# Weight sums moved between plain FFN2 tiles, one PV copy on ScalarE, and halved last stores in a sigmoid attention + SwiGLU kernel

## The chip, the cores and the metric

The kernel runs on one core of a Trainium2 chip. The metric is device time in microseconds (us) for one launch, as the median of several runs; the profile is of one execution and its span is from the first to the last instruction.

## The reference

```python
def _attn_ref(q, k, v):                       # each (8, 12, 448, 64) float32
    S = q.shape[2]
    scale = 1.0 / np.sqrt(q.shape[-1])
    scores = scale * np.matmul(q, k.transpose(0, 1, 3, 2)) - np.log(S)
    attn = 1.0 / (1.0 + np.exp(-scores))
    return np.matmul(attn, v)

x = attn_out.transpose(0, 2, 1, 3).reshape(B * S, H * D)   # (3584, 768)
g = x @ w_gate                                # (768, 1536)
silu = g * (1.0 / (1.0 + np.exp(-g)))
val = x @ w_val                               # (768, 1536)
out = silu * val @ w_out                      # (1536, 768)
```

Attention with a sigmoid in place of the softmax, over 8 batches of 12 heads, then one gated feed-forward block over all 3584 tokens.

## The kernel before, in words

**Attention.** Work goes by head groups n = 0 to 23: batch b = n // 3, four heads each. For each n and each of C = 7 chunks c of the keys, `qk_tile` makes the scores with four 64x64 matmuls (L207) and `sig_tile` takes their sigmoid on ScalarE (L225, or L222 in two halves, one per PSUM bank). When all seven chunks of an n are there, `pv` makes the product with v in 28 matmuls (L238) and three VectorE copies to the fp16 tiles xT: one of 128 partitions from the first bank (L247), two of 64 partitions from the second (L255). Only the PV of n=2, in the ramp, puts those two on ScalarE (L253). q and k come to their transposed form by DMA (`load`), a cast on GpSimd (L159) and, from n=6 on, a DMA transpose that SP issues (L167).

**FFN1.** For each batch and each of NF = 12 blocks f, `ffn1` makes gate and value in 12 matmuls (L266) into the two banks of one PSUM tile; ScalarE makes the sigmoid s (L284), VectorE the gate product t (L286) and the hidden block hT (L290).

**FFN2.** It is done for a pair of batches at once (`pb` = 0 to 3), in seven output tiles of 128 tokens by 768. Tile 6 is plain: `ffn2`, 24 matmuls (L459), two scaled copies on VectorE (L472), two stores (L479). The tiles g and g+3 are done together by `ffn2_group`, a Strassen-like form with seven half products of six matmuls each (42, L387) in place of 48. It takes sums of hidden blocks, made by `h_sums` and `make_sums` on VectorE in every odd batch (L349), and eight sums of weight blocks wT (four kinds for each of two pairs s of weight tiles), made once by `w_sum` (L319). Between products, `snap` (L398) copies a bank's partial sum out and `put` (L404) adds a bank to an output tile; TensorE goes on in the other bank meanwhile, and into the same bank only after the snapshot. The order of products is 1, 2, 6, 5, 7, 3, 4 in banks 0, 1, 0, 1, 0, 1, 0. Kinds 1 to 4 of the weight sums serve products 5, 6, 7 and 4.

**PSUM.** Four tiles of two banks are handed out in turn (`Banked`): each score tile, PV, FFN1 unit and FFN2 tile or group takes the next, so a user waits for the readers of the one four back. `read` and `write` tell the framework that work on different banks of a tile is independent. For readers of one tile on two engines that nothing is declared for, the framework puts one behind the other.

**Order.** The order of instructions on each engine is the order of the program text. A planner lays it out: `units` is a list of FFN1 blocks, weight sums and FFN2 tiles with planned durations (2.26 for an FFN1 block, 3.9 for a plain tile, 6.83 for a group, 0 for sums), and `visits` a list of attention steps of four or three chunks (visit (n, 0): chunks 0 to 3; visit (n, 4): 4 to 6), each with a due time. Before each unit, if the planned clock `tcur` has reached the due time of the next visit, that visit is put in: the score matmuls of two chunks, any PV that has become complete, the two sigmoids, then the rest (L519). A visit also brings the loads, casts and transposes of later groups (`plan`): visit (n, 0) the transposes of n+1 from n=9 on. Due times of batch 2 and after depend on the end of batch 0's FFN1 alone.

Before the change the eight weight sums stand in `units` between the FFN1 blocks of batch 1, from f=3 to f=11 (L484, L493).

**The end.** The last group of the last pair stores its first output tile o1 in two parts of 64 tokens and full width (L426) after its last product is in the program, then the second half of the columns of o2 (L430), all on SP. The first half of o2's columns is scaled by ScalarE for 64 tokens (L443) and by VectorE for the other 64 (L447), into tiles of their own, and stored from ScalarE's and SP's queues (L449).

Of the kernel before, what the change touches and what calls it, by code (L numbers as in the profile page):

```python
# [9 lines left out]
FP32 = mybir.dt.float32  # L10
# [3 lines left out]
MULT = mybir.AluOpType.mult  # L14
# [5 lines left out]
def kernel(  # L20
# [10 lines left out]
    nc = tc.nc  # L31
    ctx.enter_context(tc.manual_schedule())

    B, H, S, D = q.shape
    DM = H * D
    DFF = moe_w_gate.shape[1]
    C = S // D
# [6 lines left out]
    HREC = 1.0 / HSC  # L44
# [33 lines left out]
    class Banked:  # L78
# [28 lines left out]
        def read(self, ins, bank):  # L107
            if bank is not None:
                if self.has_mm[1 - bank]:
                    tc.declare_no_dep(ins.ins, group=self.mm[1 - bank], reason="the other bank")  # L110
                self.has_rd[bank] = True
                tc.add_to_no_dep_group(self.rd[bank], ins.ins)


    FW = 3
# [109 lines left out]
            nc.scalar.activation(out=pt, in_=sc[:, :, :S], func=SIGM, bias=sb_t, scale=qkscale)  # L225
        pts[(n, c)] = pt

    def pv(n, two=False, at=None):
        b, j = divmod(n, NJ)
        P = Banked(at=at).t  # L230
        vt = v16.pop(n)
        for c in range(C):
            pt = pts.pop((n, c))
            for h2 in range(2):
                for w in range(2):
                    r = slice(w * 64, w * 64 + 64)
                    g = (w ^ h2) * 64
                    nc.tensor.matmul(  # L238
                        out=P[g:g + 64, h2, :S],
                        lhsT=vt[r, h2, c * D:(c + 1) * D],  # L240
                        rhs=pt[r, h2, :],
                        start=(c == 0),
                        stop=(c == C - 1),
                    )

        x = xtp.tile([128, S], FP16, tag="xT", name=f"xT_{b}_{2 * j}")
        nc.vector.tensor_copy(out=x, in_=P[:, 0, :S])  # L247
        xT[(b, 2 * j)] = x
        x = xtp.tile([128, S], FP16, tag="xT", name=f"xT_{b}_{2 * j + 1}")
        for w in range(2):  # L250
            o, i = x[w * 64:(w + 1) * 64, :], P[(1 - w) * 64:(2 - w) * 64, 1, :S]
            if two:
                nc.scalar.copy(out=o, in_=i)  # L253
            else:
                nc.vector.tensor_copy(out=o, in_=i)  # L255
        xT[(b, 2 * j + 1)] = x


    hT = {}
# [88 lines left out]
                a, b, op = a12, hS[(pb, 2, i)], SUB  # L348
            nc.vector.tensor_tensor(out=t, in0=a, in1=b, op=op)  # L349

    def out_rows(pb, m):
        dsts = []
        for i in range(2):
            bb, c = divmod(2 * m + i, C)
            bb += 2 * pb
            dsts.append(out[bb * S:(bb + 1) * S, :].rearrange("(p c) n -> c p n", c=C)[c])
        return dsts

    def ffn2_group(pb, g):

        D = Banked("o")
        cs = slice(g * 128, (g + 1) * 128)

        def h_of(f, m):
            f1 = lambda i: i // FW * 2 * FW + i % FW + f
            return lambda i: (hT[(pb, f1(i))].rearrange("p b s -> p (b s)")[:, m * 128:(m + 1) * 128], f1(i))

        def s_of(kind):
            return lambda i: (hS[(pb, kind, i)][:, cs], None)

        def w_of(s, h):
            return lambda i: wo16[2 * (i // FW) + s][:, i % FW, h * hw:(h + 1) * hw]

        def t_of(kind):
            return lambda i: wT[(kind, i // FW)][:, i % FW, :]

        prods = {
            1: (h_of(0, g), w_of(0, 0)), 2: (h_of(FW, g), w_of(1, 0)), 3: (s_of(4), w_of(1, 1)),
            4: (h_of(FW, g + 3), t_of(4)), 5: (s_of(1), t_of(1)), 6: (s_of(2), t_of(2)), 7: (s_of(3), t_of(3)),
        }  # L380

        def mm(k, bank, first, last):
            A, B_ = prods[k]
            for i in range(HF):
                l, f = A(i)
                D.write(
                    nc.tensor.matmul(  # L387
                        out=D.t[:, bank, :hw], lhsT=l, rhs=B_(i), start=(first and i == 0), stop=(i == HF - 1),
                        skip_group_check=True,
                    ),  # L390
                    bank,
                    uses=(pb, f),
                )

        def snap(bank, o, half):
            o = o[:, half * hw:(half + 1) * hw]
            D.read(
                nc.vector.tensor_scalar(out=o, in0=D.t[:, bank, :hw], scalar1=HREC, scalar2=None, op0=MULT), bank  # L398
            )

        def put(bank, o, half):
            i = D.t[:, bank, :hw]
            o = o[:, half * hw:(half + 1) * hw]
            D.read(nc.vector.scalar_tensor_tensor(out=o, in0=i, scalar=HREC, in1=o, op0=MULT, op1=ADD), bank)  # L404

        last = pb == B // 2 - 1
        end = last and g == 2
        o1 = osp.tile([128, DM], FP32, tag="osb", name="osb")
        mm(1, 0, True, False)
        snap(0, o1, 0)  # L410
        mm(2, 1, True, True)
        put(1, o1, 0)
        mm(6, 0, False, False)
        snap(0, o1, 1)
        mm(5, 1, True, False)
        o2 = osp.tile([128, DM], FP32, tag="osb", name="osb")
        snap(1, o2, 1)
        mm(7, 0, False, False)
        put(0, o2, 1)
        mm(3, 1, False, True)  # L420
        put(1, o1, 1)
        mm(4, 0, False, True)
        eng = nc.sync
        dsts = out_rows(pb, g)
        for i in range(2):
            eng.dma_start(out=dsts[i], in_=o1[i * 64:(i + 1) * 64, :])  # L426
        dsts = out_rows(pb, g + 3)
        if end:
            for i in range(2):
                eng.dma_start(out=dsts[i][:, hw:], in_=o2[i * 64:(i + 1) * 64, hw:])  # L430
            last_half(D, 0, [d_[:, :hw] for d_ in dsts])
        else:
            snap(0, o2, 0)
            for i in range(2):
                eng.dma_start(out=dsts[i], in_=o2[i * 64:(i + 1) * 64, :])

    def last_half(D, bank, dsts):

        for i in range(2):
            r = slice(i * 64, i * 64 + 64)  # L440
            oe = stg.tile([128, 2, S], FP32, tag="stg", name=f"oe{i}").rearrange("p a b -> p (a b)")[:, :hw]
            if i == 0:
                ev = nc.scalar.activation(  # L443
                    out=oe[r], in_=D.t[r, bank, :hw], func=mybir.ActivationFunctionType.Copy, scale=HREC
                )
            else:
                ev = nc.vector.tensor_scalar(out=oe[r], in0=D.t[r, bank, :hw], scalar1=HREC, scalar2=None, op0=MULT)  # L447
            D.read(ev, bank)
            (nc.scalar if i == 0 else nc.sync).dma_start(out=dsts[i], in_=oe[r])  # L449

    def ffn2(pb, m):
        D = Banked("o")
# [17 lines left out]
        for half in range(2):  # L470
# [3 lines left out]
                ),  # L474
                half,
            )
        dsts = out_rows(pb, m)
        for i in range(2):
            nc.sync.dma_start(out=dsts[i], in_=osb[i * 64:(i + 1) * 64, :])  # L479


    FU1, FU2, FU3 = 2.26, 3.9, 6.83
    units = []
    t_at = {(1, 3 + i + i // 4): (i // 4, (3, 2, 1, 4)[i % 4]) for i in range(8)}  # L484
    f1_start, f1_end = {}, {}
    tt = 0.0
    for pb in range(B // 2):
        for b in (2 * pb, 2 * pb + 1):
            f1_start[b] = tt
            for f in range(NF):  # L490
                if b or f > 2:
                    units.append((FU1, ffn1, (b, f)))
                if (b, f) in t_at:  # L493
                    units.append((0.0, w_sum, t_at[(b, f)]))
                tt += FU1
            f1_end[b] = tt
        o_units = [(0.0, make_sums, (99,)), (FU2, ffn2, (pb, C - 1))]
        for g in range(3):
            o_units.append((FU3, ffn2_group, (pb, g)))
        units += o_units  # L500
        tt += sum(u[0] for u in o_units)
# [14 lines left out]
        else:  # L516
            vtime.append(FIRST + 3.5 + (b - 2 + frac) * PER)

    def attn_step(group, pvs):  # L519
        for part in (group[:2], group[2:]):  # L520
            scs = [(n, c, qk_tile(n, c)) for n, c in part]
            while pvs:
                pv(pvs.pop(0))
            for i, (n, c, sc) in enumerate(scs):

                sig_tile(n, c, sc, split=len(group) == 4 and part[0] == group[0] and i == 1)

    NPE = 2 * NJ

# [89 lines left out]
    chunk(2, 6)  # L619
    early.append(Banked("f"))  # L620
    ffn1_mm(early[1], 0, 1, range(NP - 2))
    pv(2, two=True, at=(k0 + 1) % 4)
    early.append(Banked("f", at=(k0 + 2) % 4))
    ffn1_mm(early[2], 0, 2, range(NP - 2))
    for f, Df in enumerate(early):
# [31 lines left out]
    for dur, fn, args in units:  # L657
        if vi < len(visits) and tcur >= vtime[vi]:
            group = visits[vi]
            vi += 1  # L660
            pvs, pend = pend, []
            attn_step(group, pvs)
            for n, c in group:
                for act, of in plan.get((n, c), ()):
                    act(of)
                if c == C - 1:
                    pend.append(n)
            while post:
                trans_pe(post.pop())
# [39 lines left out]
```

## Time and profile before

| what | value |
|---|---|
| three runs | 422.71, 422.71, 422.18 us |
| profiled execution | 422.16 us, span 420.4 us, clock 0.995 |
| FFN1 matmuls L266 | 1152, 353 and 352 ns each, pipelined |
| weight sums L319 | 8 in 6.2 us, 79.5 to 105.5 us |
| group matmuls L387 | 504 |
| plain tile matmuls L459 | 96, 3.9 us for 24 |
| PV copies L247, L255 | 24 and 46, 623 and 622 ns each |
| PV copies L253 on ScalarE | 2, 526 ns each |
| batch 1's FFN1, 64.6 to 102.5 us | TensorE busy 35.97 of 37.90, VectorE 31.33 |
| batch 3's FFN1, 166.9 to 201.5 us | TensorE busy 34.38 of 34.60, VectorE 24.95 |

A row of the profile names a source line, an engine and an operation, then output<-inputs by the program's names, then the shape. A matmul's length is from its start to its modelled end, and matmuls overlap, so the length of a run of them is less than their number times one. In an order of time, each row has its start, its length and, in brackets, how long its engine had stood idle and what ended that.

### The profile page before, as it was taken

Reading aid. Unit: us, or ns where it says so; the run is one execution under the profiler, and the core shown is the slowest. Engines: PE = TensorE matmul, PEld = TensorE weight load, DVE = VectorE, ACT = ScalarE, POOL = GpSimd, SP = SyncE. Lnnn points to the kernel's source line nnn. Section 1 sums busy time; section 2 is a strip of 40 time slices with the busy share of each in tenths; the row PEclk is TensorE's granted clock in tenths of the full one; section 3 lists DMA queues with packets and bytes.
Section 4 is the critical chain, followed back from the end, with each engine's and each line's share of the span. In section 5 each row is a group of like instructions: output and inputs, shape, how many; then the busy total and the mean of one; then the engine's idle time right before and its main releaser. Section 6 shows DMA issues by size and latency. Waiting matters only on the chain.

```text
span 420.4 us, 7928 instructions
## 1 busy us (share of the span) xinstructions
PE 404.7 (96%) x3189; PEld 210.7 (50%) x3189; DVE 259.8 (62%) x477; ACT 211.8 (50%) x291; POOL 95.7 (23%) x125
## 2 busy tenths in 40 slices
PE   6899999989999999999999999999999999999994
PEld 2544545445555445445555445444555544555562
DVE  2726647789565556677664556568656447578653
ACT  4976885745344565565333865665444552222000
POOL 5564242457030355030012345020000000000000
PEclk9899999999999999999999999999999999999999
DMA  8999999999469997341167998310045400000134
GB/s 299 228 274 222 212 183 224 178 215 174 124 143 236 188 163 191 84 111 23 37 122 200 179 236 209 74 24 0 2 107 144 102 2 1 2 0 2 37 95 131
DMA packets 59141, 54.39 MB, mean 129 GB/s; under 512 B 35680, under 2 KB 52448, under 8 KB 59104
## 3 DMA queue, kind: packets, MB, share of 16 engines
q0 software_dynamic: 18880, 30.94, 34.3%
q1 hardware_dynamic: 39872, 22.39, 25.9%
q8 instruction: 25, 0.41, 0.4%
q10 hardware_dynamic: 352, 0.56, 0.4%
q14 instruction: 12, 0.10, 0.1%
HBM read 47.19 MB, written 11.01 MB: 138 GB/s over the span
## 4 chain that ended last, share of the span: by engine, by line
PE 83%; DVE 7%; ACT 6%; issue 2%; DMA 1%; DVEq 0%; ACTq 0%
PE ps_D L266 47%; PE ps_D L387 19%; PE ps_D L207 7%; PE ps_D L238 7%; ACT pt L225 4%; PE ps_D L459 4%; DVE t L286 2%; DVE xT L255 1%; DVE hT L290 1%; DMA st<-in_q_dram 1%; PE ps_D L181 1%; ACT s L284 1%; DVE xT L247 1%; DVE S L349 1%; DVE wT L319 1%
## 5 line engine op out<-in xcount | busy, mean ns | idle before, releaser
L225 ACT ACTIVATE pt<-ps_D,sb_t 128x896 f16<-128x896 f32 x148 | 140.3, 1014 | 85.8 <-PE ps_D L207 85.6
L266 PE MATMUL ps_D<-xT,wg 128*128 128x448 f16 x576 | 126.9, 353 | 2.5 <-DVE t L286 1.8
L266 PE MATMUL ps_D<-xT,wv 128*128 128x448 f16 x576 | 126.4, 352 | 0.0
L286 DVE TENSOR_TENSOR t<-ps_D,s 128x448 f16<-128x448 f32 x96 | 59.8, 623 | 70.8 <-ACT s L284 70.3
L284 ACT ACTIVATE s<-ps_D 128x448 f16<-128x448 f32 x96 | 52.6, 548 | 84.8 <-PE ps_D L266 72.4
L266 PEld LDWEIGHTS <-wg 128*128 128x128 f16 x576 | 53.6, 98 | 60.5 <-issue 15.0
L266 PEld LDWEIGHTS <-wv 128*128 128x128 f16 x576 | 56.4, 98 | 52.9 <-issue 0.3
L159 POOL CAST c<-st 128x896 bf16<-128x896 f32 (+1 forms) x42 | 39.7, 956 | 128.5 <-DMA T<-c 70.7
L290 DVE SCALAR_TENSOR_TENSOR hT<-ps_D,t 128x448 f16<-128x448 f32 x96 | 60.0, 625 | 10.4 <-DVE t L286 0.5
L207 PE MATMUL ps_D<-T,T 64*64 64x448 bf16 x672 | 46.8, 361 | 3.5 <-ACT T L190 1.1
L398 DVE TENSOR_SCALAR osb<-ps_D 128x384 f32<-128x384 f32 x47 | 26.2, 558 | 21.0 <-PE ps_D L387 20.6
L387 PEld LDWEIGHTS <-S 128*128 128x128 f16 x288 | 28.2, 98 | 20.1 <-issue 1.7
L387 PE MATMUL ps_D<-wT,S 128*128 128x384 f16 x216 | 37.0, 326 | 0.8 <-DVE osb L398 0.8
L238 PE MATMUL ps_D<-pt,v 64*64 64x448 f16 x672 | 36.0, 349 | 0.5 <-ACT pt L225 0.5
L207 PEld LDWEIGHTS <-T 64*64 64x64 bf16 x672 | 16.1, 106 | 27.2 <-issue 19.8
L247 DVE CAST xT<-ps_D 128x448 f16<-128x448 f32 x24 | 15.0, 623 | 23.6 <-PE ps_D L238 18.2
L255 DVE CAST xT<-ps_D 64x448 f16<-64x448 f32 x46 | 28.6, 622 | 0.8
L404 DVE SCALAR_TENSOR_TENSOR osb<-ps_D,osb 128x384 f32<-128x384 f32 x36 | 20.1, 558 | 13.7 <-PE ps_D L387 13.3
L387 PEld LDWEIGHTS <-hT 128*128 128x128 f16 x216 | 20.5, 98 | 15.8 <-issue 2.9
L149 POOL DMA_DIRECT2D v<-in_v_dram x24 | 17.6, 731 | 41.1 <-PE ps_D L207 41.0
L238 PEld LDWEIGHTS <-v 64*64 64x64 f16 x672 | 19.8, 107 | 12.8 <-issue 1.5
L387 PE MATMUL ps_D<-wo,hT 128*128 128x384 f16 x144 | 25.4, 326 | 0.0
(40 smaller groups left out, 195.3 us busy)
## 6 DMA issues: line engine op xcount, KB each, us to landing
out_dram<-osb SPq DMA_DIRECT2D x54, 192.0 KB, 2.9
st<-in_q_dram POOLq DMA_DIRECT2D x20, 448.0 KB, 4.7
st<-in_k_dram POOLq DMA_DIRECT2D x20, 448.0 KB, 5.7
v<-in_v_dram POOLq DMA_DIRECT2D x24, 224.0 KB, 7.8
wg<-in_moe_w_gate_dram POOLq DMA_DIRECT2D x4, 576.0 KB, 14.4
wv<-in_moe_w_val_dram POOLq DMA_DIRECT2D x4, 576.0 KB, 14.6
wo<-in_moe_w_out_dram POOLq DMA_DIRECT2D x4, 576.0 KB, 11.1
st<-in_q_dram SPq DMA_DIRECT2D x4, 448.0 KB, 6.0
```

The source lines that it names most:

```text
L159: (eng.copy if eng is nc.scalar else eng.tensor_copy)(out=t.rearrange("p c h d -> p h c d"), in_=st.rearrange("p h (c d) -> p h c d", c=C) ...
L207: nc.tensor.matmul(out=sc[w * 64:(w + 1) * 64, h2, :S], lhsT=kt[r, w * 64:(w + 1) * 64], rhs=qt[r, :, w * 64:(w + 1) * 64], start=True, st ...
L225: nc.scalar.activation(out=pt, in_=sc[:, :, :S], func=SIGM, bias=sb_t, scale=qkscale)
L238: nc.tensor.matmul(out=P[g:g + 64, h2, :S], lhsT=vt[r, h2, c * D:(c + 1) * D], rhs=pt[r, h2, :], start=(c == 0), stop=(c == C - 1),)
L255: nc.vector.tensor_copy(out=o, in_=i)
L266: nc.tensor.matmul(out=D.t[:, i, :S], lhsT=w16[f // FW][:, pr, cs], rhs=xT[(b, pr)], start=(pr == 0), stop=(pr == NP - 1),),
L284: D.read(nc.scalar.activation(out=s16, in_=D.t[:, 0, :S], func=SIGM), 0)
L286: D.read(nc.vector.tensor_tensor(out=t1, in0=D.t[:, 0, :S], in1=s16, op=MULT), 0)
L290: nc.vector.scalar_tensor_tensor(out=hT[(b // 2, f)][:, b % 2, :], in0=D.t[:, 1, :S], scalar=HSC, in1=t1, op0=MULT, op1=MULT),
L387: nc.tensor.matmul(out=D.t[:, bank, :hw], lhsT=l, rhs=B_(i), start=(first and i == 0), stop=(i == HF - 1), skip_group_check=True,),
L398: nc.vector.tensor_scalar(out=o, in0=D.t[:, bank, :hw], scalar1=HREC, scalar2=None, op0=MULT), bank
L404: D.read(nc.vector.scalar_tensor_tensor(out=o, in0=i, scalar=HREC, in1=o, op0=MULT, op1=ADD), bank)
```

## The change: what it does

Four edits, in one diff.

- The weight sums leave FFN1 of batch 1. FFN2 of the first pair now has three plain tiles (6, 0, 3) and the groups 1 and 2 only. Three sums stand after tile 6, three after tile 0, two after tile 3, ahead of group 1. Groups stay as they are in the other pairs.
- `pv` takes `how`: 0 puts all three copies on VectorE, 2 both half copies on ScalarE (the PV of n=2, as before), 1 one half copy on ScalarE, after the sigmoids of the step's first two chunks. A visit ahead of an FFN1 block uses 0, any other visit 1.
- `apart` declares that a reader of a PSUM tile need not stand behind named readers of it (another bank or other partitions). It is used for `how` = 1 and for the last two scaled copies.
- In the last group, o1 is stored in two halves of columns: the first after `put(1, o1, 0)`, the second at the end. The half of o2 is stored right after `put(0, o2, 1)`.

```diff
+    def apart(second, *firsts):
+        for first in firsts:
+            keys[0] += 1
+            tc.add_to_no_dep_group(f"half{keys[0]}", first.ins)
+            tc.declare_no_dep(second.ins, group=f"half{keys[0]}", reason="another bank or other partitions")
...
-        nc.vector.tensor_copy(out=x, in_=P[:, 0, :S])
+        first = nc.vector.tensor_copy(out=x, in_=P[:, 0, :S])
...
+        halves = [(x[w * 64:(w + 1) * 64, :], P[(1 - w) * 64:(2 - w) * 64, 1, :S]) for w in range(2)]
+        done = [nc.vector.tensor_copy(out=o, in_=i) for o, i in halves[how:]]
+        if how == 2:
+            for o, i in halves:
                 nc.scalar.copy(out=o, in_=i)
...
+        def rest():
+            if how == 1:
+                o, i = halves[0]
+                apart(nc.scalar.copy(out=o, in_=i), first, *done)
+
+        return rest
...
         put(1, o1, 0)
+        if end:
+            store((nc.sync, nc.sync), pb, g, o1, lo)
         mm(6, 0, False, False)
         snap(0, o1, 1)
...
         put(0, o2, 1)
+        if end:
+            store((nc.sync, nc.sync), pb, g + 3, o2, hi)
         mm(3, 1, False, True)
         put(1, o1, 1)
         mm(4, 0, False, True)
...
+        store((nc.sync, nc.sync), pb, g, o1, hi)
...
+            store_half(nc.scalar if w == 0 else nc.sync, pb, g + 3, w, oe, lo)
+        apart(evs[1], evs[0])
...
-    t_at = {(1, 3 + i + i // 4): (i // 4, (3, 2, 1, 4)[i % 4]) for i in range(8)}
...
-                if (b, f) in t_at:
-                    units.append((0.0, w_sum, t_at[(b, f)]))
...
         o_units = [(0.0, make_sums, (99,)), (FU2, ffn2, (pb, C - 1))]
-        for g in range(3):
+        if pb == 0:
+            ts = [(0.0, w_sum, (s, kind)) for s in range(2) for kind in (3, 2, 1, 4)]
+            o_units += ts[:3] + [(FU2, ffn2, (pb, 0))] + ts[3:6] + [(FU2, ffn2, (pb, 3))] + ts[6:]
+        for g in range(1 if pb == 0 else 0, 3):
             o_units.append((FU3, ffn2_group, (pb, g)))
...
             scs = [(n, c, qk_tile(n, c)) for n, c in part]
-            while pvs:
-                pv(pvs.pop(0))
+            rest = [pv(pvs.pop(0), how) for _ in range(len(pvs))]
             for i, (n, c, sc) in enumerate(scs):
                 sig_tile(n, c, sc, split=len(group) == 4 and part[0] == group[0] and i == 1)
+            for f in rest:
+                f()
...
-    pv(2, two=True, at=(k0 + 1) % 4)
+    pv(2, how=2, at=(k0 + 1) % 4)
...
-            attn_step(group, pvs)
+            attn_step(group, pvs, 0 if fn is ffn1 else 1)
```

More of the change, by code (lines that the diff above doesn't have):

```diff
@@ L226, in sig_tile, with pv @@
         pts[(n, c)] = pt
-    def pv(n, two=False, at=None):
+    def pv(n, how=0, at=None):
         b, j = divmod(n, NJ)
@@ L246, in pv @@
         x = xtp.tile([128, S], FP16, tag="xT", name=f"xT_{b}_{2 * j}")
-        nc.vector.tensor_copy(out=x, in_=P[:, 0, :S])
+        first = nc.vector.tensor_copy(out=x, in_=P[:, 0, :S])
         xT[(b, 2 * j)] = x
         x = xtp.tile([128, S], FP16, tag="xT", name=f"xT_{b}_{2 * j + 1}")
-        for w in range(2):
-            o, i = x[w * 64:(w + 1) * 64, :], P[(1 - w) * 64:(2 - w) * 64, 1, :S]
-            if two:
-                nc.scalar.copy(out=o, in_=i)
-            else:
-                nc.vector.tensor_copy(out=o, in_=i)
-        xT[(b, 2 * j + 1)] = x
+        xT[(b, 2 * j + 1)] = x
+        halves = [(x[w * 64:(w + 1) * 64, :], P[(1 - w) * 64:(2 - w) * 64, 1, :S]) for w in range(2)]
+        done = [nc.vector.tensor_copy(out=o, in_=i) for o, i in halves[how:]]
+        if how == 2:
+            for o, i in halves:
+                nc.scalar.copy(out=o, in_=i)
+        def rest():
[3 more added lines that the diff above has]
+        return rest
     hT = {}
@@ L349, in make_sums, with store, store_half @@
             nc.vector.tensor_tensor(out=t, in0=a, in1=b, op=op)
[L351 to L357, printed above, removed]
+    def store(engs, pb, m, osb, cols):
+        for w in range(2):
+            store_half(engs[w], pb, m, w, osb, cols)
+    def store_half(eng, pb, m, w, osb, cols):
+        bb, c = divmod(2 * m + w, C)
+        bb += 2 * pb
+        d = out[bb * S:(bb + 1) * S, cols].rearrange("(p c) n -> c p n", c=C)[c]
+        eng.dma_start(out=d, in_=osb[w * 64:(w + 1) * 64, cols])
     def ffn2_group(pb, g):
@@ L404, in put @@
             D.read(nc.vector.scalar_tensor_tensor(out=o, in0=i, scalar=HREC, in1=o, op0=MULT, op1=ADD), bank)
-        last = pb == B // 2 - 1
-        end = last and g == 2
+        end = pb == B // 2 - 1 and g == 2
+        lo, hi, both = slice(0, hw), slice(hw, DM), slice(0, DM)
         o1 = osp.tile([128, DM], FP32, tag="osb", name="osb")
@@ L422, in ffn2_group @@
         mm(4, 0, False, True)
[L423 to L432, printed above, removed]
-            snap(0, o2, 0)
[L434 to L442, printed above, removed]
+        if not end:
+            store((nc.sync, nc.sync), pb, g, o1, both)
+            snap(0, o2, 0)
+            store((nc.sync, nc.sync), pb, g + 3, o2, both)
+            return
+        store((nc.sync, nc.sync), pb, g, o1, hi)
+        evs = []
+        for w in range(2):
+            r = slice(w * 64, w * 64 + 64)
+            oe = stg.tile([128, 2, S], FP32, tag="stg", name=f"oe{w}").rearrange("p a b -> p (a b)")
+            if w == 0:
                 ev = nc.scalar.activation(
-                    out=oe[r], in_=D.t[r, bank, :hw], func=mybir.ActivationFunctionType.Copy, scale=HREC
+                    out=oe[r, :hw], in_=D.t[r, 0, :hw], func=mybir.ActivationFunctionType.Copy, scale=HREC
                 )
             else:
-                ev = nc.vector.tensor_scalar(out=oe[r], in0=D.t[r, bank, :hw], scalar1=HREC, scalar2=None, op0=MULT)
-            D.read(ev, bank)
-            (nc.scalar if i == 0 else nc.sync).dma_start(out=dsts[i], in_=oe[r])
+                ev = nc.vector.tensor_scalar(out=oe[r, :hw], in0=D.t[r, 0, :hw], scalar1=HREC, scalar2=None, op0=MULT)
+            D.read(ev, 0)
+            evs.append(ev)
+            store_half(nc.scalar if w == 0 else nc.sync, pb, g + 3, w, oe, lo)
+        apart(evs[1], evs[0])
     def ffn2(pb, m):
@@ L476, in ffn2 @@
             )
-        dsts = out_rows(pb, m)
-        for i in range(2):
-            nc.sync.dma_start(out=dsts[i], in_=osb[i * 64:(i + 1) * 64, :])
+        store((nc.sync, nc.sync), pb, m, osb, slice(0, DM))
     FU1, FU2, FU3 = 2.26, 3.9, 6.83
     units = []
-    t_at = {(1, 3 + i + i // 4): (i // 4, (3, 2, 1, 4)[i % 4]) for i in range(8)}
     f1_start, f1_end = {}, {}
@@ L517, with attn_step @@
             vtime.append(FIRST + 3.5 + (b - 2 + frac) * PER)
-    def attn_step(group, pvs):
+    def attn_step(group, pvs, how):
         for part in (group[:2], group[2:]):
             scs = [(n, c, qk_tile(n, c)) for n, c in part]
-            while pvs:
-                pv(pvs.pop(0))
+            rest = [pv(pvs.pop(0), how) for _ in range(len(pvs))]
             for i, (n, c, sc) in enumerate(scs):
                 sig_tile(n, c, sc, split=len(group) == 4 and part[0] == group[0] and i == 1)
+            for f in rest:
+                f()
     NPE = 2 * NJ
```

## The prediction

> **What bounds the kernel now.** I read the page's busy times and its chain first, then the wait table of TensorE (PE), then the order of time around each of its waits, then the tail. The busy row and the chain:
>
> ```profile
> PE 404.7 (96%) x3189; PEld 210.7 (50%) x3189; DVE 259.8 (62%) x477; ACT 211.8 (50%) x291; POOL 95.7 (23%) x125
> PE 83%; DVE 7%; ACT 6%; issue 2%; DMA 1%; DVEq 0%; ACTq 0%
> ```
>
> TensorE is busy for 96% of the 420.4 us span and carries 83% of the chain. So there are only three ways to move the time: matmuls added or removed, idle holes of TensorE closed or opened, and the stretch after the last matmul. The wait table gives the holes; these three lines are those after the ramp that come from VectorE (DVE), in total us, count, longest (a fourth, of 0.2, is in the ramp):
>
> ```profile
> PE ps_D L266 <- DVE t L286: 1.8, 3, 1.3
> PE ps_D L387 <- DVE osb L398: 0.8, 4, 0.2
> PE ps_D L207 <- DVE hT L290: 0.6, 1, 0.6
> ```
>
> Where they lie: 0.60 at 81.6 and 1.33 at 91.1, both in FFN1 of batch 1; 0.24, 0.18, 0.17 and 0.24 in FFN2 (118.7, 216.8, 308.1, 325.3); 0.22 at 170.3 and at 235.0. That is 3.2 us in all. The two large ones in order of time (start, length, instruction, idle before it in brackets):
>
> ```profile
> 79.50 0.75 DVE L319 TENSOR_TENSOR wT<-wo,wo 128x1152 f16<-128x1152 f16 x1
> ...
> 81.57 0.57 PE L207 MATMUL ps_D<-T,T 64*64 64x448 bf16 x8 [0.60 <-DVE hT L290]
> ...
> 89.74 0.75 DVE L319 TENSOR_TENSOR wT<-wo,wT 128x1152 f16<-128x1152 f16 x1
> 90.41 0.62 DVE L286 TENSOR_TENSOR t<-ps_D,s 128x448 f16<-128x448 f32 x1
> 91.08 1.29 PE L266 MATMUL ps_D<-xT,wg 128*128 128x448 f16 x6 [1.33 <-DVE t L286]
> ```
>
> A weight sum (wT) stands on VectorE just ahead of the gate product t or hT that TensorE needs before it may refill a PSUM tile. From 77 to 91 us VectorE is busy 12.9 of 14.0 us, and four sums (4 x 0.75 = 3.0) are part of that. The FFN2 hole and the tail:
>
> ```profile
> 116.76 1.26 DVE L255 CAST xT<-ps_D 64x448 f16<-64x448 f32 x2
> 118.05 0.56 DVE L398 TENSOR_SCALAR osb<-ps_D 128x384 f32<-128x384 f32 x1
> ...
> 118.66 3.08 PE L387 MATMUL ps_D<-wT,S 128*128 128x384 f16 x18 [0.24 <-DVE osb L398]
> ```
> ```profile
> 415.56 0.55 ACTq L449 DMA_DIRECT2D out_dram<-oe  x1
> 415.62 0.56 DVE L447 TENSOR_SCALAR oe<-ps_D 64x384 f32<-64x384 f32 x1 [1.04 <-ACT oe L443]
> 415.77 1.25 SPq L430 DMA_DIRECT2D out_dram<-osb  x2
> 417.12 0.54 SPq L449 DMA_DIRECT2D out_dram<-oe  x1
> ```
>
> In the first, the snapshot L398 stands behind three PV copies of 0.62. In the second, the last store leaves SP at 417.12, behind four others (two of L426 from 414.61, two of L430); it lands 2.2 us later, and the span ends 1.05 after that.
>
> **What the Trainium skill says.** "PSUM — Partial Sum Buffer", section "Engine vs sequencer instructions": ScalarE and VectorE queues are strict FIFO. The trace agrees: L398 runs only after the copies ahead of it. Same page, "PSUM bank collisions raise a hardware error": two engines may be in one bank at once if they touch different 32-partition quadrants. The new paired readers do, since each takes 64 partitions; no row of before shows such a pair together (DVE L447 waits 1.04 for ACT L443). "DMA: Bandwidth & Descriptors", section "Issuing engines are not separate DMA queues": several issuers save only issue time. In the tail that is 0.47 to 0.62 a store on SP.
>
> **The change part by part**, against the span of 420.4.
>
> 1. *Weight sums leave batch 1: −1.93.* All eight (6.2 us of L319) go. First hole: without the sum at 79.50, t and hT end 0.7 earlier, near 80.85, and TensorE is busy with PV until 80.97: hole 0. Second: with four sums fewer ahead of it, t is bound by its sigmoid instead. Following the rows: QK at 80.97, its sigmoids to 83.4, then s, t, hT and two S sums (0.36 each) per unit bring the t in question to its end near 88.7, while TensorE would want it at 89.15. Hole 0, slack 0.4. So 0.60 + 1.33 = 1.93 (bounds 0.9 and 1.93). The inputs keep up: the tightest operand of this stage, the transposed k of n=7, landed 5.6 us before use.
>
> 2. *Three plain tiles: +0.97.* Group 0 of the first pair (7 products x 6 = 42 matmuls) becomes tiles 0 and 3 (2 x 24 = 48). A plain tile takes 3.90 us in the chain (L459 x24), a group 6.83: 2 x 3.90 − 6.83 = +0.97, all on TensorE. VectorE evacuations fall from seven of 0.56 to four of 0.55, which is beside it. SP gets four stores of 192 KB either way.
>
> 3. *The sums' new place: +0.84.* Six of eight run on VectorE while TensorE has 3.9 us per tile for 2 x 0.55 of evacuation: 1.1 + 3 x 0.75 = 3.35 fits, at no cost. The last two (kinds 1 and 4 of the second pair) do not. Working through the planner, visit (9,0), with PV of n=8, falls just before them. So VectorE's queue reads PV copy, PV half copy, sum, sum, snapshot L398, and TensorE's third product waits for that snapshot. By the rows at 116: first copy from 116.10 to 116.73, half copy to 117.38, two sums to 118.88, L398 to 119.45, TensorE at 119.5. It could start at 118.66 − 0.24 = 118.42. Hole 1.08 in place of 0.24: +0.84. Queued behind it are only the following put and snapshots, which catch up inside the group. Bounds 0.3 and 1.1.
>
> 4. *One PV half copy on ScalarE in FFN2: −0.59.* Three of the four PVs there lose 0.62 on VectorE, more than the holes of 0.18, 0.17, 0.24 (the fourth is in 3). On ScalarE the copy costs 0.53 (row L253); it stands behind the split sigmoid and delays the next two by 0.53. Their PSUM tiles are wanted only after a tile or group of 4 to 7 us, and the timeline shows ScalarE idle 4.8 to 8.7 before each of these visits. Cost 0, bounds 0 and 0.2.
>
> 5. *The planner's clock: +0.4.* The extra 0.97 is added to tcur after FFN2 of pair 0, while due times stay. A visit moves up when its lateness at the unit before was negative by less than 0.97. Visits (11,0), (11,4), (13,0), (13,4), (17,0), (17,4), (19,0), (19,4), the lone last PV by one FFN1 unit; (15,0) by one group; (21,0) past ffn2. Their transposes, SP's queue included, have slack of 6.6 us and more, except n=17: k landed at 237.78 for a use at 239.58. That visit (due 162.39; tcur 161.78 a unit earlier becomes 162.75) now wants it at 237.22, that is 5.6 us after the first of its two transposes is issued (231.60, behind FFN2's last stores). That pair took 6.2; the five other pairs issued behind stores took 4.8 to 6.4. So bounds 0 and 0.8, value 0.4. For (21,0), QK could wait up to 0.2 on the last hT; I take 0. The two holes of 0.22 stay.
>
> 6. *Tail: −1.1.* The first half of o1 is stored at about 410.9 and o2's half at 413.6, under matmuls. After 414.6 SP issues two half stores of o1 (to about 416.0), then the last one at 416.05 instead of 417.12; the DVE reading no longer waits for ACT (from 415.05 instead of 415.62) and is ready by then. It lands at 418.27 by its own 2.2; ACT's store landed at 418.23. Before: 419.34. So 1.07 earlier (bounds 0.8 and 1.3).
>
> Sum: −1.93 + 0.97 + 0.84 − 0.59 + 0.4 − 1.1 = **−1.4**: span 419.0. That profiled execution took 422.16 with its span of 420.4; the three timed runs are 422.71, 422.71 and 422.18. I apply it to the median: **421.3**.
>
> **The rivals.** *A, batch 1 has a second limiter.* If t is then held by its sigmoid behind three score sigmoids (2.8 us on ScalarE), only about half of 1.93 comes back: −0.4, 422.3, no change that can be told. For it: ScalarE's idle before s is short there (0.6 to 1.7). Against: the estimate left 0.4 of slack, and later odd batches, with the same sums of h and no wT, show one hole of 0.22.
>
> *B, slower: the early half store holds its own tile.* L398's second snapshot writes the other columns of o1 while the store of the first columns is in flight. If the program orders them as one tile, that snapshot waits for the landing: second half issued near 411.4, landing 2.6 later, 414.0, instead of starting at 411.10. TensorE's product 7 waits for it: +2.7, total +1.3, **424.0**. It decides only if the wait is there at all; the columns are disjoint, and no row of before has a write to a part of a tile whose other part a DMA is reading.
>
> *C, less is lost.* The n=17 transposes land in time, and the sums cost their lower bound: −0.4 − 0.54 more: −2.3, 420.4.
>
> *D, moved visits open holes that I priced at 0* (at (21,0), (19,0), or a late load): +1.5 or more beyond the forecast, 422.8 and up.
>
> **How the numbers follow.** About 0.2% (0.85 us) can be told from no change. Forecast 0.55, A 0.17, B 0.08, C 0.12, D 0.08. Faster: forecast and C, 0.67. Slower: B and half of D, 0.12. Same: the rest, 0.21. The range leaves out B and D's far end. Low end: C, the tail's 1.3 in place of 1.1, and half of the 0.5 between the three runs: 420.36 − 0.2 − 0.25 = 419.9. High end: A with step 5 at its 0.8 and step 4 at its 0.2: 422.3 + 0.4 + 0.2 = 422.9.
>
> **What would show it.** No L319 rows before FFN2 and no VectorE waits of TensorE between 77 and 92; 144 of L459's matmuls instead of 96; a TensorE wait on the osb snapshot near 1.1 in the first group after the plain tiles and none at the other three FFN2 visits; a TensorE wait on T of 0 to 0.8 before visit (17,0); SP's last store about 1.1 after the last matmul instead of 2.1. I am wrong if the batch 1 holes remain, if the snapshot wait of step 3 is absent or twice as long, or if an L398 in the last group waits on a DMA.

## The result, and the profile after

| | before | changed |
|---|---|---|
| median of 4 runs | 422.63 us | 420.6 us (419.93 to 421.21) |
| ratio, 95% interval | | 0.9954 [0.9937, 0.9971] |
| span of the profiled execution | 420.4 us | 418.2 us |

The changed kernel is faster by about half a per cent; a second measurement on another occasion gave 420.69 against 422.83, 0.9946 [0.9933, 0.9959]. One of its six executions of the changed kernel took 845.59 us and is left out of that ratio; its cause was not sought. The range held the result (419.9 to 422.9); the forecast of 421.3 was 0.7 us high. Line numbers shift in the changed kernel: L404 is the group matmul (L387 before), L280 FFN1 (L266), L214 the scores (L207), L474 the plain tile (L459), L333 the weight sum (L319), L415 the snapshot (L398), L421 the put (L404 before), L300 and L304 are t and hT, L260 and L268 the half copies on VectorE and ScalarE, L487 the plain tile's evacuation, L363 the sums of h.

The page's busy row and chain of the changed kernel:

```profile
PE 405.9 (97%) x3195; PEld 211.2 (50%) x3195; DVE 255.9 (61%) x470; ACT 214.3 (51%) x295; POOL 95.2 (23%) x125
PE 89%; ACT 4%; DVE 3%; issue 1%; DMA 1%; DVEq 0%; ACTq 0%
```

TensorE has six matmuls more, and VectorE's share of the chain fell from 7% to 3%. The table of TensorE's waits (us in total, times, longest) has two lines left from VectorE that lie after the ramp (the start-up, up to 65 us):

```profile
PE ps_D L404 <- DVE osb L415: 0.9, 1, 0.9
PE ps_D L280 <- DVE t L300: 0.4, 2, 0.2
```

Both waits of batch 1 are gone. In order of time (start, length, instruction), the same two places as shown of before:

```profile
80.38 0.62 DVE L304 SCALAR_TENSOR_TENSOR hT<-ps_D,t 128x448 f16<-128x448 f32 x1
...
81.06 0.57 PE L214 MATMUL ps_D<-T,T 64*64 64x448 bf16 x8
...
88.22 0.62 DVE L300 TENSOR_TENSOR t<-ps_D,s 128x448 f16<-128x448 f32 x1
88.48 0.76 PE L214 MATMUL ps_D<-T,T 64*64 64x448 bf16 x12
```

hT ends at 81.00, where PV leaves TensorE at about the same time, and t ends at 88.84, 0.3 before TensorE has done its scores. No bracket with an idle time stands on either matmul row. The first group after the plain tiles:

```profile
115.80 0.62 DVE L260 CAST xT<-ps_D 64x448 f16<-64x448 f32 x1
116.23 1.91 ACT L232 ACTIVATE pt<-ps_D,sb_t 128x896 f16<-128x896 f32 x2
116.43 0.76 DVE L333 TENSOR_TENSOR wT<-wo 128x1152 f16<-128x1152 f16 x1
117.11 0.75 DVE L333 TENSOR_TENSOR wT<-wo,wT 128x1152 f16<-128x1152 f16 x1
117.77 0.55 DVE L415 TENSOR_SCALAR osb<-ps_D 128x384 f32<-128x384 f32 x1
118.38 3.08 PE L404 MATMUL ps_D<-wT,S 128*128 128x384 f16 x18 [0.88 <-DVE osb L415]
```

This is the new hole: two weight sums stand between the half copy and the snapshot that the third product waits for. The tail:

```profile
413.99 0.48 ACT L456 ACTIVATE oe<-ps_D 64x384 f32<-64x384 f32 x1 [25.01 <-PE ps_D L404]
414.00 0.56 DVE L460 TENSOR_SCALAR oe<-ps_D 64x384 f32<-64x384 f32 x1 [0.47 <-PE ps_D L404]
414.51 0.55 ACTq L374 DMA_DIRECT2D out_dram<-oe  x1
415.07 0.55 SPq L374 DMA_DIRECT2D out_dram<-oe  x1
```

The two readers, in one bank and on 64 partitions each, start together, and SP's last store leaves 1.2 us after the last matmul (413.91) where it was 2.2.

### A ledger by stage

The stages are cut at first score matmuls of a visit, which do the same work in all kernels. "Ramp" ends at visit (6,0), "batch 1" at (8,4), "plain" at (9,0), "group" at (9,4), "FFN2 p1" runs from (14,4) to (16,0), "b 4, 5" to (20,4), "FFN2 p2" to (22,4), "tail" from the last matmul's end. Stages left out are equal within 0.01. First column: length before, in us of the profiled span; the others: what each kernel adds to it, each from one execution.

| stage | before | changed | e1 | e2 | e3 | e4 | e5 | e6 | e7 | e8 | e9 |
|---|---|---|---|---|---|---|---|---|---|---|---|
| ramp | 64.62 | +0.16 | +0.93 | −0.28 | −0.06 | +0.70 | +0.86 | +0.84 | +0.37 | −0.22 | +0.09 |
| batch 1 | 41.84 | −2.05 | −2.05 | +0.64 | +0.32 | −2.06 | −1.96 | −2.05 | −2.05 | +10.86 | +0.33 |
| plain | 7.62 | +0.98 | +0.97 | 0.00 | +0.07 | +0.98 | +0.98 | +0.98 | +0.97 | 0.00 | 0.00 |
| group | 9.54 | +0.64 | +1.25 | −0.40 | 0.00 | −0.40 | +1.25 | +0.64 | −0.40 | −0.40 | 0.00 |
| FFN2 p1 | 28.63 | −0.34 | +0.05 | −0.33 | 0.00 | −0.33 | +0.05 | −0.09 | −0.09 | −0.33 | 0.00 |
| b 4, 5 | 64.96 | +0.08 | +0.08 | 0.00 | 0.00 | +0.07 | +0.08 | 0.00 | 0.00 | 0.00 | 0.00 |
| FFN2 p2 | 35.88 | −0.51 | −0.34 | −0.74 | 0.00 | −0.52 | −0.33 | −0.74 | −0.74 | −0.74 | 0.00 |
| tail | 5.43 | −1.18 | −0.04 | −0.03 | −1.16 | −1.19 | −1.20 | −1.19 | −1.20 | −1.18 | +0.03 |

The changed column sums to −2.2, the difference of the spans. No edit touches what the ramp does, and yet it moves by −0.3 to +0.9 between these executions, nearly all of it within the first 17 us; so single spans are compared from the ramp's end, and whole kernels by their ratios. It is longer in all six kernels with the sums moved (+0.16 to +0.93) than in the other five (−0.28 to +0.09). With one trace of each, it stays open whether that is chance; if it is not, the moved sums are worth less than their stages say.

### The profile page after: what moved, and what is told of

Read it like the earlier page. It is cut to its first block, busy times and chain, and to the rows that moved or that the text cites. A ratio compares the mean times of both kernels' runs of the same rounds, so it can differ in the third digit from the quotient of the medians.

```text
span 418.2 us, 7945 instructions
## 1 busy us (share of the span) xinstructions
PE 405.9 (97%) x3195; PEld 211.2 (50%) x3195; DVE 255.9 (61%) x470; ACT 214.3 (51%) x295; POOL 95.2 (23%) x125
## 4 chain that ended last, share of the span: by engine, by line
PE 89%; ACT 4%; DVE 3%; issue 1%; DMA 1%; DVEq 0%; ACTq 0%
PE ps_D L280 50%; PE ps_D L404 18%; PE ps_D L214 8%; PE ps_D L246 7%; PE ps_D L474 6%; ACT pt L232 3%; PE ps_D L188 1%; DMA st<-in_q_dram 1%; DVE t L300 1%; ACT s L298 1%; DVE xT L255 1%; DVE hT L304 0%; DVE xT L260 0%; ACT pt L229 0%; DVE T L197 0%
## 5 line engine op out<-in xcount | busy, mean ns | idle before, releaser
L280 PE MATMUL ps_D<-xT,wg 128*128 128x448 f16 x576 | 126.9, 353 | 1.1 <-ACT pt L232 0.5
L280 PE MATMUL ps_D<-xT,wv 128*128 128x448 f16 x576 | 126.4, 352 | 0.0
L300 DVE TENSOR_TENSOR t<-ps_D,s 128x448 f16<-128x448 f32 x96 | 59.8, 623 | 74.9 <-ACT s L298 74.6
L280 PEld LDWEIGHTS <-wg 128*128 128x128 f16 x576 | 53.5, 98 | 59.3 <-issue 13.7
L280 PEld LDWEIGHTS <-wv 128*128 128x128 f16 x576 | 56.4, 98 | 52.8 <-issue 0.3
L304 DVE SCALAR_TENSOR_TENSOR hT<-ps_D,t 128x448 f16<-128x448 f32 x96 | 60.0, 625 | 10.4 <-DVE t L300 0.5
L214 PE MATMUL ps_D<-T,T 64*64 64x448 bf16 x672 | 47.8, 369 | 2.4 <-ACT T L197 1.1
L415 DVE TENSOR_SCALAR osb<-ps_D 128x384 f32<-128x384 f32 x43 | 24.0, 558 | 19.0 <-PE ps_D L404 18.1
L404 PEld LDWEIGHTS <-S 128*128 128x128 f16 x264 | 25.8, 98 | 18.1 <-issue 1.1
L404 PE MATMUL ps_D<-wT,S 128*128 128x384 f16 x198 | 34.0, 326 | 0.9 <-DVE osb L415 0.9
L214 PEld LDWEIGHTS <-T 64*64 64x64 bf16 x672 | 16.2, 107 | 26.6 <-issue 19.1
L260 DVE CAST xT<-ps_D 64x448 f16<-64x448 f32 x42 | 26.1, 621 | 0.7
L421 DVE SCALAR_TENSOR_TENSOR osb<-ps_D,osb 128x384 f32<-128x384 f32 x33 | 18.4, 558 | 13.2 <-PE ps_D L404 13.1
L404 PEld LDWEIGHTS <-hT 128*128 128x128 f16 x198 | 18.9, 98 | 14.2 <-issue 2.1
L474 PE MATMUL ps_D<-wo,hT 128*128 128x384 f16 x144 | 24.2, 326 | 0.0
```

The lines of the kernel that those rows point to most:

```text
L214: nc.tensor.matmul(out=sc[w * 64:(w + 1) * 64, h2, :S], lhsT=kt[r, w * 64:(w + 1) * 64], rhs=qt[r, :, w * 64:(w + 1) * 64], start=True, st ...
L260: done = [nc.vector.tensor_copy(out=o, in_=i) for o, i in halves[how:]]
L280: nc.tensor.matmul(out=D.t[:, i, :S], lhsT=w16[f // FW][:, pr, cs], rhs=xT[(b, pr)], start=(pr == 0), stop=(pr == NP - 1),),
L300: D.read(nc.vector.tensor_tensor(out=t1, in0=D.t[:, 0, :S], in1=s16, op=MULT), 0)
L304: nc.vector.scalar_tensor_tensor(out=hT[(b // 2, f)][:, b % 2, :], in0=D.t[:, 1, :S], scalar=HSC, in1=t1, op0=MULT, op1=MULT),
L404: nc.tensor.matmul(out=D.t[:, bank, :hw], lhsT=l, rhs=B_(i), start=(first and i == 0), stop=(i == HF - 1), skip_group_check=True,),
```

## The experiments

All ratios are to the kernel before, with their 95% intervals.

**e1: the sums alone.** The kernel before with this part of the change only.

```diff
-                if (b, f) in t_at:
-                    units.append((0.0, w_sum, t_at[(b, f)]))
...
+            o_units += ts[:3] + [(FU2, ffn2, (pb, 0))] + ts[3:6] + [(FU2, ffn2, (pb, 3))] + ts[6:]
```

> The kernel before with only the weight sums moved (three plain tiles in the first pair; all three PV copies on VectorE everywhere; tail as before). Theory, the parts add up as stage by stage in the two traces: batch 1 gives 2.06 us back, the plain tiles cost 0.98, and the first group after them waits for its snapshot behind three copies and two sums, so its hole is 0.88 + 0.62 = about 1.5 where it was 0.24; with 0.28 for moved visits the whole is +0.3 to +0.6 us, no gain. Rival, the moved sums are the main gain of the change and the copy only tidies up: -1.0 us or better.

Measured: 422.95 us, 0.9998 [0.9990, 1.0006]: no difference. Batch 1 gives the whole 2.05 back, and 0.97 for the plain tiles and 1.25 for the first group take it away. From the ramp's end the trace stands at −0.08, where +0.3 to +0.6 was expected: moving visit (21,0) ahead of the plain tile did not cost 0.2 but closed the hole at 308.1 (FFN2 p2, −0.34). TensorE's waits and the row of that group:

```profile
PE ps_D L387 <- DVE osb L398: 2.0, 3, 1.5
```
```profile
119.76 1.46 PE L387 MATMUL ps_D<-wT,S 128*128 128x384 f16 x8 [1.49 <-DVE osb L398]
```

One wait of 1.5 is the longest of three: three PV copies and two sums ahead of one snapshot. The moved sums are no gain by themselves; the rival falls.

**e2: the copy alone.** The kernel before with `how` = 1 at FFN2 visits.

```diff
-        for w in range(2):
...
-                nc.vector.tensor_copy(out=o, in_=i)
...
+        done = [nc.vector.tensor_copy(out=o, in_=i) for o, i in halves[how:]]
...
+                apart(nc.scalar.copy(out=o, in_=i), first, *done)
```

> The kernel before with only one PV half copy on ScalarE at FFN2 visits (sums and tail as before). Theory, a hole of TensorE costs about 0.16 us more than the idle time that the wait table lists, since that idle time is counted from the modelled end of the last matmul: the four holes of 0.24, 0.18, 0.17, 0.24 close and give 0.41 + 0.34 + 0.34 + 0.41 = 1.5 us. Rival, the listed idle time is the cost: 0.83 us. ScalarE's later sigmoids cost nothing in either.

Measured: 421.25 us, 0.9966 [0.9954, 0.9978], about 1.4 us less. By stages the rows group, FFN2 p1 and FFN2 p2 give 0.40 + 0.33 + 0.74 = 1.47, as the theory had it and not the 0.83 that the wait table lists. Why, is seen in the changed kernel at the same visit as before's 325.27:

```profile
322.25 2.12 PE L404 MATMUL ps_D<-wo,hT 128*128 128x384 f16 x12
...
323.49 0.56 DVE L415 TENSOR_SCALAR osb<-ps_D 128x384 f32<-128x384 f32 x1
...
324.21 3.09 PE L404 MATMUL ps_D<-wT,S 128*128 128x384 f16 x18
```

Without a hole the next product starts 1.96 after the run's start, 0.16 before the run's modelled end (322.25 + 2.12). With the hole of before it started 2.37 after (322.90 to 325.27): the hole cost 0.41, and the table listed 0.24.

From the ramp's end the profiled execution gained only 0.86, because batch 1 lost 0.64 in it. This is not the edit, which touches no visit of batch 1; e3 and e9, which also keep the sums there, lost 0.32 and 0.33. Its cause is in e2's order of time:

```profile
97.18 0.94 POOL L166 CAST c<-st 128x896 bf16<-128x896 f32 x1 [1.88 <-DMA st<-in_q_dram]
97.24 1.48 DVE L333 TENSOR_TENSOR wT<-wT,wo 128x1152 f16<-128x1152 f16 x1
...
100.04 0.57 PE L214 MATMUL ps_D<-T,T 64*64 64x448 bf16 x8 [0.50 <-DVE hT L304]
```

The sum took 1.48 us instead of 0.75 beside a GpSimd cast that began just before it. Where the cast falls depends on when a load lands, so batch 1 with sums in it differs between executions; with the sums gone it is −2.05 or −2.06 in five of six kernels. The trace of before, which the ledger is counted from, has the shortest batch 1 of the four with sums on VectorE.

**e3 and e9: the tail, whole and its readers alone.** e3 takes all tail edits and no other; e9 only this:

```diff
+        evs = []
...
+            evs.append(ev)
...
+        apart(evs[1], evs[0])
```

> The kernel before with only the tail changed (o1 in two halves, o2's half earlier, the last two readers side by side). Theory, SP's queue of stores sets the end: the stretch from TensorE's last matmul to the end of the span falls from 5.4 to 4.3 us, -1.1 us. Rival, the landing of ScalarE's own store sets it: -0.5 us or less.

> The kernel before with only the last two readers set side by side (no store moved). Theory, SP's queue of stores sets the end, and VectorE's reader has over 1 us of slack there: the stretch after the last matmul stays at 5.4 us, no change. Rival, the 1.04 us wait of the VectorE reader is part of the path: -0.5 us.

Measured: e3 421.91 us, 0.9982 [0.9970, 0.9993], tail 1.16 shorter; e9 422.98 us, 1.0003 [0.9991, 1.0015], tail +0.03. Both rivals fall: the wait of 1.04 of the VectorE reader was never on the path; the stores in SP's queue were.

**e4: the sums four and four.** The changed kernel with

```diff
-            o_units += ts[:3] + [(FU2, ffn2, (pb, 0))] + ts[3:6] + [(FU2, ffn2, (pb, 3))] + ts[6:]
+            o_units += ts[:4] + [(FU2, ffn2, (pb, 0))] + ts[4:] + [(FU2, ffn2, (pb, 3))]
```

> The changed kernel with the weight sums placed four and four, after the first and the second plain tile, none after the third. Theory, the two sums between the PV copies and the snapshot are the whole of the new hole: the listed wait of 0.88 goes to 0 and the time is 1.0 us less than the changed kernel's, about 3.1 us under the kernel before. Rival, the two sums only move the lag: VectorE then starts the last plain tile's evacuation late, scores wait for its PSUM tile, and less than 0.4 us is gained.

Measured: 419.41 us, 0.9920 [0.9908, 0.9933]. The group's row goes from +0.64 to −0.40, 1.04 as expected. VectorE's and TensorE's rows there:

```profile
112.81 0.75 DVE L333 TENSOR_TENSOR wT<-wo,wT 128x1152 f16<-128x1152 f16 x1
113.70 0.57 PE L214 MATMUL ps_D<-T,T 64*64 64x448 bf16 x8
113.72 1.02 DVE L487 TENSOR_SCALAR osb<-ps_D 128x384 f32<-128x384 f32 x2 [0.16 <-PE ps_D L474]
...
117.17 0.56 DVE L415 TENSOR_SCALAR osb<-ps_D 128x384 f32<-128x384 f32 x1 [0.21 <-PE ps_D L404]
117.87 1.30 PE L404 MATMUL ps_D<-wT,S 128*128 128x384 f16 x7
```

The fourth sum ends 0.16 before the last plain tile is ready to be taken out, so nothing is late, and the snapshot now waits for TensorE instead of the other way round.

**e5: the copies back on VectorE.** The changed kernel with `attn_step(group, pvs, 0)` everywhere.

> The changed kernel with all three PV copies back on VectorE at FFN2 visits. Theory: the hole after the plain tiles grows by 0.62, those of the second pair and of the third pair's second visit come back (0.34 and 0.41), the third pair's first visit has moved ahead of the plain tile and shows none: +1.4 us over the changed kernel, -0.7 against the kernel before. Rival, copies and sums do not share a path and only the old holes come back: +0.8.

Measured: 421.89 us, 0.9969 [0.9954, 0.9983]; from the ramp's end 1.24 more than the changed kernel, where +1.4 was expected and +0.8 by the rival. The group's row is +1.25, as in e1, against +0.64 with the copy; FFN2 p1 loses 0.39. FFN2 p2 loses only 0.18, in two parts: its first hole stays closed without the copy, since visit (21,0) has moved ahead of the plain tile, and the 0.23 that the changed kernel loses at (21,0) (step 5 below) did not come here (first part −0.33, against −0.11); its second hole is open again (0.00, against −0.40).

**e6 and e7: the planner's clock as before.** The changed kernel, and e4, with

```diff
-            o_units += ts[:3] + [(FU2, ffn2, (pb, 0))] + ts[3:6] + [(FU2, ffn2, (pb, 3))] + ts[6:]
+            o_units += ts[:3] + [(FU3 / 2, ffn2, (pb, 0))] + ts[3:6] + [(FU3 / 2, ffn2, (pb, 3))] + ts[6:]
```

These are e6's lines; e7 has the same two planned times in e4's order.

> The changed kernel with the two new plain tiles planned at 3.415 in place of 3.9, so that the planner's clock after the first pair, and every later visit, stands as before. Theory: the moved visits cost only the two small waits seen in the changed kernel's trace, 0.07 at visit (17,0) and 0.2 at (21,0): -0.2 to -0.3 us against the changed kernel. Rival, the prediction's size with a late transpose of n=17: -0.4; or they cost nothing: 0.

> Both of the two: sums four and four, and the planner's clock as before. If the two parts are independent the time is 1.3 us under the changed kernel's, 3.3 under the kernel before. If the earlier visits hid something else, less.

Measured: e6 420.5 us, 0.9932 [0.9915, 0.9949]; e7 419.03 us, 0.9902 [0.9885, 0.9919]. The costs of moved visits vanish as expected (+0.08 and the 0.23 of p2), but FFN2 p1 gives back 0.25 in both. In e6 VectorE stood still there ahead of the snapshot, and no other engine is named (more on this under step 5 below):

```profile
216.48 0.56 DVE L415 TENSOR_SCALAR osb<-ps_D 128x384 f32<-128x384 f32 x1 [0.55 <-issue]
...
217.09 3.08 PE L404 MATMUL ps_D<-wT,S 128*128 128x384 f16 x18
```

From the ramp's end e6 is 0.07 and e7 0.05 shorter than its partner, where 0.2 to 0.3 was expected: where visits stand is worth nothing that these runs can tell. e4 and e7 are the fastest here: their intervals overlap and end at 0.9933 and 0.9919, where the two of the changed kernel begin at 0.9937 and 0.9933.

**e8: the sums on GpSimd.** At their old places in batch 1, all groups kept, the changed copies and tail.

```diff
-        nc.vector.tensor_tensor(out=t, in0=a, in1=b, op=op)
+        nc.gpsimd.tensor_tensor(out=t, in0=a, in1=b, op=op)
```

> The weight sums at their old places in batch 1 but on GpSimd in place of VectorE, all groups kept, with the changed copies and tail. Theory that VectorE's load alone made the holes of batch 1: they close, no plain tiles are paid and no sum stands ahead of a snapshot: -2.06 - 1.5 - 1.1 = -4.7 us against the kernel before. Rival: GpSimd's queue, which also casts and issues the loads, falls behind (a cast of 896 elements takes it 0.96 us, a sum reads twice 1152), or VectorE's own instructions get slower beside it; then transposes or gates come late in batch 1 and half or all of the gain is lost.

Measured: 430.86 us, 1.0204 [1.0173, 1.0235]: slower. Everything but batch 1 gains as expected (the rows group to tail), and batch 1 loses 10.86: the rival holds, by VectorE's own instructions getting slower. In order of time:

```profile
74.67 2.38 POOL L333 TENSOR_TENSOR wT<-wT,wo 128x1152 f16<-128x1152 f16 x1
75.42 8.38 DVE L363 TENSOR_TENSOR S<-hT 128x384 f16<-128x384 f16 x1
...
76.99 2.37 POOL L333 TENSOR_TENSOR wT<-wo 128x1152 f16<-128x1152 f16 x1
...
79.31 2.36 POOL L333 TENSOR_TENSOR wT<-wo,wT 128x1152 f16<-128x1152 f16 x1
...
85.12 2.83 PE L246 MATMUL ps_D<-pt,v 64*64 64x448 f16 x28 [5.21 <-DVE hT L304]
```

A sum of h on VectorE, 0.36 us elsewhere, took 8.38 while GpSimd ran three weight sums and then issued three loads. TensorE stood 5.2 us behind it. The Trainium skill, "SBUF — State Buffer", section "Who interferes with whom", says that a VectorE instruction with two SBUF inputs contends with a GpSimd instruction that reads SBUF, and calls the shared port pair an exclusive lock. The traces agree: in the eleven of the ledger, 37 VectorE sums with both inputs in SBUF were drawn out (sums of h over 0.5 us, weight sums over 0.85), and each ran beside a GpSimd instruction that had begun before it; t and hT, with one input from PSUM, kept their 0.62 in e8. The 8.38 adds that VectorE can be held over several GpSimd instructions in a row, the three load issues included.

## Why the prediction was right, point by point

| step | forecast | measured, from the ledger |
|---|---|---|
| 1 sums leave batch 1 | −1.93 | −2.05 |
| 2 three plain tiles | +0.97 | +0.98 |
| 3 the sums' new place | +0.84 | +0.64 |
| 4 copy on ScalarE, elsewhere in FFN2 | −0.59 | −1.08 |
| 5 the planner's clock | +0.4 | +0.31 |
| 6 tail | −1.1 | −1.18 |
| sum | −1.4 | −2.4, and +0.16 in the ramp |

Steps 1, 2 and 6 hold in sign, place and size; e1 (−2.05, +0.97) shows the first two without the copy and the tail, e3 (−1.16) the tail alone. Step 1 gave 0.12 more than the 1.93 that the prediction took for its upper bound, the sum of two listed waits. e9 adds to step 6 that the side-by-side readers give nothing without the moved stores. One reading of the prediction was incomplete: the ramp holds three more waits of TensorE for VectorE (1.2, 0.6 and 0.5), on which no step rests.

**The term that was mis-sized is step 4.** It took the listed idle times 0.18, 0.17 and 0.24 for the cost of the three holes. They cost 0.33, 0.34 and 0.40 (e2), since TensorE pipelines and a hole is listed only from the modelled end of the last matmul. That is 0.5 of the 1.0 us by which the sum was short. The measured −1.08 is FFN2 p1's −0.34 and −0.74 for FFN2 p2, which is its −0.51 without the +0.23 that the table gives to step 5. It counts the hole at 308.1 as closed by the copy, which e2 does show; but the moved visit (21,0) closes it without the copy as well (FFN2 p2 is −0.34 in e1 and −0.33 in e5), so in the changed kernel 0.33 of it could as well be given to step 5.

Step 3 had the right rows in the right order. Its sums were counted at their length of 0.75, but one starts 0.66 to 0.68 after the other; that, twice, and short gaps are the 0.2. Removing those two sums (e4) gave the whole hole back, and taking the copy away from it added 0.61 (e5). So steps 3 and 4 share one path: the copy is worth more with the sums there than without (0.61 against 0.40), and the parts cannot be added blindly.

Step 5 came near its number by luck; its mechanism failed. The transposes of n=17 took 5.2 us from issue to landing in the changed kernel, not 6.2, and landed 0.5 us before use, so the wait that was priced at 0.4 did not come. What the table has in its place is 0.08 at visit (17,0) and 0.23 at (21,0). The latter was named as up to 0.2 and taken as 0; there hT started 0.46 late on VectorE:

```profile
299.32 0.62 DVE L300 TENSOR_TENSOR t<-ps_D,s 128x448 f16<-128x448 f32 x1
...
300.40 0.62 DVE L304 SCALAR_TENSOR_TENSOR hT<-ps_D,t 128x448 f16<-128x448 f32 x1 [0.46 <-DVE t L300]
...
301.07 0.57 PE L214 MATMUL ps_D<-T,T 64*64 64x448 bf16 x8
```

This is no price of the move. Every trace of the ledger has one such standstill of VectorE after the ramp, of 0.46 to 0.56 us, which the profile puts down to no other engine, and it stands at a fixed count of VectorE's instructions (semaphore instructions counted): ahead of the 448th in before, changed, e3, e4 and e9, of the 576th in e1, e2, e5 and e8, of the 320th in e6 and e7. In the changed kernel and in e4 it meets visit (21,0), and TensorE waits; in e1 and e5, with the same order of visits, it comes at 383 us and the 0.23 does not. In e6 and e7 it meets the snapshot of FFN2 p1 and costs 0.25 there. So taking the move back gained 0.07 (e6), and not the 0.31 of the table.

Of the rivals, A (a second limiter in batch 1) falls: no wait of TensorE is left there. B falls: the changed kernel's snapshot into the other half of o1 started at 410.05, 0.42 after its product as everywhere, while the store of the first half, issued at 409.92, landed at 412.49. C was right that the transposes come in time; the median lies nearer to its 420.4 than to the forecast, but not by its way, since the sums cost 0.64 and not its 0.3. D happened in small, at (21,0).

## What to carry to other kernels

A wait's listed idle time can understate what a pipelined engine loses, here by 0.16 us for a hole in FFN2: measure the distance from start to start of the same work with and without the hole. When work is moved off a crowded queue, list what it then stands ahead of: here two sums of 0.7 between a copy and a snapshot undid half of the 2 us won, and moving them one slot up gave the two fastest kernels (e4, e7). An edit that shows nothing alone (e1) can be worth keeping once the work that it collides with is moved.

## What the runs showed of the hardware that was not expected

- A VectorE sum of two SBUF tensors took 8.38 us instead of 0.36 beside GpSimd's sums (e8), and 1.48 instead of 0.75 beside a single GpSimd cast (e2).
- The same sum on GpSimd took 2.37 us, on VectorE 0.75.
- VectorE stood still once in every trace for about half a microsecond (0.46 at 299.9 in the changed kernel, 0.55 in e6 at 215.9), at its 320th, 448th or 576th instruction, which are 128 apart. What it waits for there was not tried.
- The first 65 us of the kernel varied by 1.2 us between the traces with the same work in them, and did so within the first 17 us.
